# Ones for the warm-up, and V's first weights on ScalarE's queue: a transformer block of layer norm, sliding-window attention and a gated MLP

## The chip, the cores and the metric

The kernel runs on one core of a Trainium2 chip. The time is device microseconds of one execution, from the first to the last instruction; "before" is the median of three runs. The core has five engines with an instruction stream each: TensorE (PE, matmuls; its weight loads are listed as PEld), VectorE (DVE), ScalarE (ACT), GpSimd (POOL) and SyncE (SP), which here only issues DMA transfers. SBUF is the on-chip memory of 128 partitions, PSUM the memory into which TensorE accumulates, HBM the memory outside.

## The reference

For x of shape [1, 2048, 640] in bf16, with 32 heads of 20 channels and a window of 256 keys:

```python
def reference(A_x, A_wqkv, A_wo, B_x, B_w_gate, B_w_up, B_w_down):
    x = A_x
    xn = _layernorm(x, axis=-1)                  # mean, variance, eps 1e-5
    # _A_ref: q, k, v = xn @ wqkv;  scores = q k^T * Dh**-0.5
    #         mask: 0 <= i - j < 256;  softmax;  (p @ v) @ wo
    # _B_ref: h = sigmoid(xn @ w_gate) * (xn @ w_up);  h @ w_down
    return x + _A_ref(xn, A_wqkv, A_wo) + _B_ref(xn, B_w_gate, B_w_up, B_w_down)
```

Attention and MLP both read the same normalised rows, and the input is added to their sum.

## The kernel before

The sequence is worked through in four chunks of 512 rows, each of four blocks of 128 rows. Only the start of the kernel is touched by the change: the loads of chunk 0, the warm-up, the layer norm of chunk 0 and its V projection. First the warm-up tile and the loads, all on SyncE's queue, in program order:

```python
    warm = stp.tile([P, CW], BF16, name="st")          # 128 x 512
    nc.vector.memset(warm, 0.0)
    ...
    def load_rows(s, queue):                            # one block of x, 160 KB
        queue.dma_start(out=xc[0][:, s, :], in_=xr[:, s, :])

    def load_v(hf):                                     # 320 columns of wqkv, 400 KB
        a = 2 * D + hf * HALF
        nc.sync.dma_start(out=wqkv[:, :, a:a + HALF], in_=wqkv_r[:, :, a:a + HALF])

    load_rows(0, nc.sync)
    load_rows(1, nc.sync)
    load_v(0)
    load_rows(3, nc.sync)
    load_rows(2, nc.sync)
    load_v(1)
    load_wqkv(0)
    load_wqkv(1)
```

Then come constants, a first activation (so that ScalarE's table is loaded early) and ten matmuls of 128 x 512, whose result nobody reads. They keep TensorE busy until the first data are there:

```python
    make_identity(nc, ident)
    ...
    nc.scalar.activation(out=scr, in_=eps, func=SQRT)
    for n in (6, 4):
        ps = ps_d.tile([P, CW], FP32, name="pwarm", tag="d")
        for k in range(n):
            nc.tensor.matmul(ps, lhsT=warm[:, 0:P], rhs=warm, start=(k == 0), stop=(k == n - 1))
```

The layer norm of chunk 0 is shared by two engines. VectorE makes the statistics of blocks 0 and 2, ScalarE those of blocks 1 and 3; ScalarE takes every square root, VectorE every normalisation. TensorE transposes a normalised block by five matmuls with the identity, VectorE copies the result out of PSUM, and five matmuls of 320 columns project half of V for that block. The order below is the order of each engine's own stream:

```python
    mv0 = ln_block(0, 0)                 # VectorE: statistics of block 0
    xn1, neg1 = mean_act(1)              # ScalarE: mean of block 1
    r0 = root(mv0)                       # ScalarE: square root for block 0
    r1 = root_act(1, xn1, neg1)          # ScalarE: squares and root for block 1
    norm(0, mv0, r0)                     # VectorE: reciprocal, normalise block 0
    for lo, hi in ((0, 3), (3, DC)):
        transpose_rows(0, dve, lo, hi)   # TensorE transposes, VectorE copies
    v00 = project_v(0, 0, 0)             # TensorE: first half of V, block 0
    norm_act(1, xn1, neg1, r1)           # VectorE: normalise block 1
    xn3, neg3 = mean_act(3)
    r3 = root_act(3, xn3, neg3)
    half2 = ln_half(0, 2, 0)
    transpose_rows(1, dve)
    mv2 = ln_mv(ln_half(0, 2, 1, half2))
    v10 = project_v(0, 1, 0)             # first half of V, block 1
    copy_v(0, 0, 0, v00, act)
    r2 = root(mv2)
    v01 = project_v(0, 0, 1)             # second half of V, block 0
    norm_act(3, xn3, neg3, r3)
    norm(2, mv2, r2)
    ...                                  # blocks 3 and 2, then Q and K of chunk 0
```

After this, Q, K, the MLP, the scores and the products with V follow as one list of matmuls into which the attention steps are mixed.

Of the kernel before, what the change touches and what calls it, by code (L numbers as in the profile page):

```python
# [9 lines left out]
P = 128  # L10
# [7 lines left out]
CW = 512  # L18
# [6 lines left out]
HALF = 320  # L25
# [9 lines left out]
BF16 = mybir.dt.bfloat16  # L35
# [72 lines left out]
def kernel(  # L108
# [11 lines left out]
    nc = tc.nc  # L120
# [4 lines left out]
    def pool(name, bufs, **kw):  # L125
        return ctx.enter_context(tc.tile_pool(name=name, bufs=bufs, **kw))
# [5 lines left out]
    stp = pool("stp", 5)  # L132
# [23 lines left out]
    wqkv = const.tile([P, DC, 3 * D], BF16, name="wqkv")  # L156
    wqkv_r = A_wqkv.rearrange("(c p) n -> p c n", p=P)
# [2 lines left out]
    wd = const.tile([P, FC, D], BF16, name="wd")  # L160
    wo = const.tile([P, DC, D], BF16, name="wo")

    warm = stp.tile([P, CW], BF16, name="st")
    nc.vector.memset(warm, 0.0)
    def load_wqkv(part):
        nc.sync.dma_start(out=wqkv[:, :, part * D:(part + 1) * D],
                          in_=wqkv_r[:, :, part * D:(part + 1) * D])
# [3 lines left out]
    def load_rows(s, queue):  # L171
        queue.dma_start(out=xc[0][:, s, :], in_=xr[:, s, :])  # L172

    def load_v(hf):
        a = 2 * D + hf * HALF
        nc.sync.dma_start(out=wqkv[:, :, a:a + HALF], in_=wqkv_r[:, :, a:a + HALF])

    load_rows(0, nc.sync)
    load_rows(1, nc.sync)
    load_v(0)  # L180
    load_rows(3, nc.sync)
    load_rows(2, nc.sync)
    load_v(1)
    load_wqkv(0)
    load_wqkv(1)

# [49 lines left out]
    for n in (6, 4):  # L236
        ps = ps_d.tile([P, CW], FP32, name="pwarm", tag="d")
        for k in range(n):
            nc.tensor.matmul(ps, lhsT=warm[:, 0:P], rhs=warm, start=(k == 0), stop=(k == n - 1))


    xnT = {}
# [542 lines left out]
```

## Time and profile before

| | us |
|---|---|
| median of three runs | 313.3 |
| lowest, highest | 313.13, 313.94 |
| span in the profile | 311.7 |
| TensorE busy | 306.7 (98%) |
| ScalarE busy | 192.1 (62%) |
| VectorE busy | 159.9 (51%) |
| GpSimd busy | 155.5 (50%) |

In the views that follow, a line of the timeline has the start in us, the length in us, the engine, the line of the kernel and its operation, what it writes and reads with shapes, and in brackets how long the engine stood idle before and who ended that. Several instructions of one line that follow one another are merged, with their number after an x. A line of the chain has the start, the length and the work. SPq and ACTq are the issuing of transfers by SyncE and ScalarE. Matmuls are pipelined, so one matmul's length is more than the distance to the start of the next. Line 172 of the kernel loads a block of x, 176 half of V's weights, 239 is the warm-up, 248 and 254 are VectorE's statistics, 599 to 605 those of ScalarE, 589 the root, 268 and 610 the normalisations, 275 and 276 the transposes and their copies, 322 the V projection, 295 Q and K.

### The profile page before, as it was taken

What the parts mean: (1) busy time and instruction counts of PE and PEld (TensorE: products, weight loads), DVE (VectorE), ACT (ScalarE), POOL (GpSimd) and SP (SyncE); (2) the same over time, 40 slices, a digit from 0 to 9 for tenths busy, and PEclk for the clock granted to TensorE, in tenths of its full rate; (3) what the DMA queues carried; (4) which work ended last, traced back from release to release, by engine and by line L of the source; (5) the groups of instructions that cost most, each with busy time, mean ns of one, the idle gap of its engine ahead of it and who ended that gap; (6) DMA issues with size and microseconds to landing.
All of it is one profiled execution on the core that took longest, in us unless ns stands there. A gap on an engine that the chain in (4) does not pass through costs nothing.

```text
span 311.7 us, 10549 instructions
## 1 busy us (share of the span) xinstructions
PE 306.7 (98%) x4663; PEld 175.7 (56%) x4663; DVE 159.9 (51%) x315; ACT 192.1 (62%) x178; POOL 155.5 (50%) x239
## 2 busy tenths in 40 slices
PE   8999999999999999999999999999999999999996
PEld 3654444556557655644567665644556675444774
DVE  4533746648695264289826155262723526272423
ACT  5614787697764648787673647768585547778000
POOL 3000676576872827567382627546372845556000
PEclk9999999999999999999999999999999999999999
DMA  7995999574663153630025212730000223000002
GB/s 200 370 366 166 310 381 196 210 187 133 207 79 106 44 157 98 211 107 2 2 44 86 87 57 91 224 116 2 2 3 2 67 64 109 0 4 0 4 21 65
DMA packets 37614, 35.71 MB, mean 115 GB/s; under 512 B 10272, under 2 KB 37024, under 8 KB 37536
## 3 DMA queue, kind: packets, MB, share of 16 engines
q1 hardware_dynamic: 37280, 34.92, 38.5%
q8 instruction: 36, 0.59, 0.8%
q10 hardware_dynamic: 288, 0.11, 0.1%
q14 instruction: 10, 0.08, 0.1%
HBM read 23.63 MB, written 10.26 MB: 109 GB/s over the span
## 4 chain that ended last, share of the span: by engine, by line
PE 97%; DMA 2%; DVE 0%; SPq 0%; issue 0%; DVEq 0%
PE y L422 17%; PE pu L408 17%; PE pg L401 17%; PE pqk L295 14%; PE ps L472 9%; PE pv L322 7%; PE y L429 7%; PE acc L504 7%; DMA wqkv<-in_A_wqkv_dram 2%; PE pt L275 0%; SPq L172 0%; DVE h L412 0%; DVE xnT L276 0%; DVE xn L433 0%; DVEq L412 0%
## 5 line engine op out<-in xcount | busy, mean ns | idle before, releaser
L480 POOL TENSOR_SCALAR_AFFINE_SELECT pT<-pT 128x512 bf16<-128x512 bf16 (+2 forms) x192 | 147.0, 796 | 129.1 <-ACT pT L477 129.0
L477 ACT ACTIVATE pT<-ps 128x2048 bf16<-128x2048 f32 x76 | 142.7, 1878 | 64.0 <-PE ps L472 59.4
L412 DVE SCALAR_TENSOR_TENSOR h<-th,pu 128x512 bf16<-128x512 f32 x48 | 32.6, 682 | 60.5 <-PE pu L408 47.5
L408 PE MATMUL pu<-xnT,wu 128*128 128x512 bf16 x240 | 59.8, 380 | 0.0
L401 PE MATMUL pg<-xnT,wg 128*128 128x512 bf16 x240 | 59.8, 380 | 0.0
L422 PE MATMUL y<-wd,h 128*128 128x320 bf16 (+2 forms) x396 | 57.0, 296 | 0.0
L295 PE MATMUL pqk<-xnT,wqkv 128*128 128x512 bf16 x200 | 46.0, 381 | 0.0
L422 PEld LDWEIGHTS <-h 128*128 128x128 bf16 x396 | 36.5, 98 | 14.3
L404 ACT ACTIVATE th<-pg 128x512 f32<-128x512 f32 x48 | 28.6, 596 | 14.6 <-PE pg L401 14.3
L401 PEld LDWEIGHTS <-wg 128*128 128x128 bf16 x240 | 22.3, 98 | 25.3 <-issue 0.2
L408 PEld LDWEIGHTS <-wu 128*128 128x128 bf16 x240 | 21.9, 98 | 25.5 <-issue 0.6
L472 PEld LDWEIGHTS <-kT 20*64 20x64 bf16 x1856 | 20.6, 104 | 24.2 <-issue 22.3
L295 PEld LDWEIGHTS <-wqkv 128*128 128x128 bf16 x200 | 22.5, 119 | 18.0 <-issue 0.6
L472 PE MATMUL ps<-qT,kT 20*64 20x128 bf16 (+4 forms) x1856 | 32.5, 239 | 0.0
L433 DVE SCALAR_TENSOR_TENSOR rows<-y,rows 128x320 bf16<-128x320 f32 x30 | 14.5, 489 | 33.3 <-PE y L429 30.0
L514 DVE STREAM_TRANSPOSE t<-acc 128x512 f32<-128x512 f32 x32 | 22.0, 710 | 18.5 <-PE acc L504 18.2
L526 DVE TENSOR_TENSOR on<-t,rec 128x320 bf16<-128x320 f32 (+4 forms) x48 | 27.5, 573 | 1.1
L322 PE MATMUL pv<-wqkv,xnT 128*128 128x320 bf16 x160 | 23.9, 302 | 0.8 <-DVE xnT L276 0.6
L429 PE MATMUL y<-wo,oc 128*128 128x320 bf16 (+2 forms) x165 | 24.2, 295 | 0.0
L504 PE MATMUL acc<-pT,v 128*32 128x64 bf16 (+3 forms) x1376 | 23.2, 223 | 0.1
L504 PEld LDWEIGHTS <-v 128*32 128x32 bf16 x1376 | 18.6, 97 | 7.9 <-issue 1.9
L322 PEld LDWEIGHTS <-xnT 128*128 128x128 bf16 x160 | 15.0, 99 | 7.5 <-DVE xnT L276 1.3
(45 smaller groups left out, 134.0 us busy)
## 6 DMA issues: line engine op xcount, KB each, us to landing
qT<-sq SPq DMA_DIRECT2D x7, 512.0 KB, 5.9
sq<-st SPq DMA_DIRECT2D x20, 128.0 KB, 3.0
sk<-st SPq DMA_DIRECT2D x20, 128.0 KB, 3.1
rows<-in_A_x_dram SPq DMA_DIRECT2D x15, 160.0 KB, 2.3
out_dram<-rows SPq DMA_DIRECT2D x15, 160.0 KB, 1.8
kT<-sk SPq DMA_DIRECT2D x4, 512.0 KB, 6.4
wg<-in_B_w_gate_dram SPq DMA_DIRECT2D x2, 960.0 KB
wu<-in_B_w_up_dram SPq DMA_DIRECT2D x2, 960.0 KB, 9.9
```

Of the source, the lines that this page charges most:

```text
L295: nc.tensor.matmul(ps, lhsT=wt[:, m, :], rhs=xnT[c][:, d, :], start=(d == 0), stop=(d == DC - 1))
L322: nc.tensor.matmul(ps[:, 0:HALF], lhsT=xnT[c][:, d, s * P:(s + 1) * P], rhs=wqkv[:, d, 2 * D + hf * HALF:2 * D + (hf + 1) * HALF], start=( ...
L401: nc.tensor.matmul(pg, lhsT=part(wg, d, f), rhs=xnT[c][:, d, :], start=(d == 0), stop=(d == DC - 1))
L404: nc.scalar.activation(out=th, in_=pg, func=TANH, scale=0.5)
L408: nc.tensor.matmul(pu, lhsT=part(wu, d, f), rhs=xnT[c][:, d, :], start=(d == 0), stop=(d == DC - 1))
L412: nc.vector.scalar_tensor_tensor(out=h, in0=th, scalar=1.0, in1=pu, op0=ADD, op1=MULT)
L422: nc.tensor.matmul(y[:, 0:cut[1] - cut[0]], lhsT=ht[c, f][:, s * P:(s + 1) * P], rhs=wd[:, f, cut[0]:cut[1]], start=(f == 0), stop=False)
L429: nc.tensor.matmul(y[:, 0:cut[1] - cut[0]], lhsT=oc[c, m][:, s * P:(s + 1) * P], rhs=wo[:, m, cut[0]:cut[1]], start=False, stop=(m == DC - 1))
L472: nc.tensor.matmul(ps[hf * U:(hf + 1) * U, i, col * U:(col + n) * U], lhsT=qk["k", kc, g // GH][32 * i:32 * i + DH, g % GH, key:key + U], ...
L477: nc.scalar.activation(out=pt[:, :, 0:CW], in_=ps, func=EXP, scale=SCALE)
L480: nc.gpsimd.affine_select(out=out, in_=in_, pattern=[[0, HG], [0, n], [sign, width]], compare_op=GE, fill=0.0, base=base, channel_multipli ...
L504: nc.tensor.matmul(acc[32 * i:32 * i + 32, q * U:(q + n) * U], lhsT=v[:, h * VW:h * VW + 32], rhs=pt[:, i, col * U:(col + n) * U], start=( ...
```

## The change

Two things are done at the start of the kernel. The warm-up matmuls read a constant of ones that the program has anyway, one element per partition read again for every column, in place of a tile that VectorE must first clear; so they have nothing of their own to wait for. And the first half of V's weights is issued by ScalarE, as its first instruction, beside SyncE's issue of the first block of x, and not as the third transfer on SyncE's queue; the first V projection is to have its weights sooner. The other transfers stay on SyncE in the same order.

```diff
-    warm = stp.tile([P, CW], BF16, name="st")
-    nc.vector.memset(warm, 0.0)
+    ones = nc.const_aps.tensor(1.0, [P, CW], BF16)
...
-    def load_v(hf):
+    def load_v(hf, queue):
         a = 2 * D + hf * HALF
-        nc.sync.dma_start(out=wqkv[:, :, a:a + HALF], in_=wqkv_r[:, :, a:a + HALF])
+        queue.dma_start(out=wqkv[:, :, a:a + HALF], in_=wqkv_r[:, :, a:a + HALF])

     load_rows(0, nc.sync)
     load_rows(1, nc.sync)
-    load_v(0)
+    load_v(0, nc.scalar)
     load_rows(3, nc.sync)
     load_rows(2, nc.sync)
-    load_v(1)
+    load_v(1, nc.sync)
     load_wqkv(0)
     load_wqkv(1)
...
-            nc.tensor.matmul(ps, lhsT=warm[:, 0:P], rhs=warm, start=(k == 0), stop=(k == n - 1))
+            nc.tensor.matmul(ps, lhsT=ones[:, 0:P], rhs=ones, start=(k == 0), stop=(k == n - 1))
```

## The prediction

> **What bounds the kernel now.** I read the page first: the shares of busy time, the forty slices and the chain of work that ended last.
>
> ```profile
> PE 306.7 (98%) x4663; PEld 175.7 (56%) x4663; DVE 159.9 (51%) x315; ACT 192.1 (62%) x178; POOL 155.5 (50%) x239
> PE   8999999999999999999999999999999999999996
> DMA  7995999574663153630025212730000223000002
> PE 97%; DMA 2%; DVE 0%; SPq 0%; issue 0%; DVEq 0%
> ```
>
> TensorE is busy for 306.7 of 311.7 us and carries 97% of the chain. Nothing in the change touches those matmuls. What is not TensorE on the chain lies in the first slices, so the second view is the chain of the first 40 us, in order of time (start, length, what).
>
> ```profile
> 0.80 0.40 SPq L172
> 1.25 0.42 SPq L172
> 1.72 4.72 DMA wqkv<-in_A_wqkv_dram
> 6.47 1.19 PE pv L322 x5
> 7.66 0.29 PE pt L275 x5
> 7.98 0.50 DVE xnT L276
> 8.53 1.53 PE pv L322 x10
> 14.01 10.79 PE pqk L295 x50
> ```
>
> The first useful TensorE work that isn't a transpose is V's first half for block 0, at 6.47 us. The chain gives its wait to V's first 400 KB, issued third on SyncE's queue at 1.72 and landing 4.72 us later, at 6.44. From 8.53 us on TensorE hardly stops: from 8.50 to 13.85 it is busy 5.33 of 5.35 us. So the end moves almost one for one with the start of this dense stretch at 8.53. Third view: the timeline of the first microseconds, for what else ends just before 6.47.
>
> ```profile
> 0.92 0.27 DVE L164 MEMSET st<- 128x256 uint32 x1 [0.92 <-PEq L769]
> 1.25 4.45 PE L239 MATMUL pwarm<-st 128*128 128x512 bf16 x10 [1.25 <-DVE st L164]
> 3.13 0.88 DVE L248 BATCH_NORM_STATS2 stats<-xc 128x6 f32<-128x320 bf16 x2 [1.94 <-DMA xc<-in_A_x_dram]
> 3.63 0.74 ACT L599 ACTIVATE xn<-xc 128x640 bf16<-128x640 bf16 x1 [0.63 <-DMA xc<-in_A_x_dram]
> 4.37 0.28 ACT L589 ACTIVATE rstd<-mv,eps 128x1 f32<-128x1 f32 x1
> 4.88 0.45 DVE L268 TENSOR_SCALAR xn<-xc,mv,rstd 128x640 bf16<-128x640 bf16 x1
> 5.50 0.74 PE L275 MATMUL pt<-ident,xn 128*128 128x128 bf16 x5
> 6.06 0.55 DVE L276 COPY xnT<-pt 128x384 bf16<-128x384 bf16 x2 [0.73 <-PE pt L275]
> 6.47 0.85 PEld L322 LDWEIGHTS <-xnT 128*128 128x128 bf16 x5 [0.51 <-DVE xnT L276]
> 6.47 1.19 PE L322 MATMUL pv<-wqkv,xnT 128*128 128x320 bf16 x5 [0.24 <-DMA wqkv<-in_A_wqkv_dram]
> ```
>
> The last two lines are the point. The weight load of the same matmul also starts at 6.47, and it waited 0.51 us for the transposed block from VectorE. The matmul has two releasers which come within a few hundredths of each other: V's landing (6.44) and the layer norm of x's first block. Removing one leaves the other.
>
> That second chain starts with x, not with V. Block 0 lands by 3.13, block 1 by 3.63. ScalarE works in order: it takes the mean of block 1 (3.63, with its accumulator read out from 4.27) ahead of the root of block 0 (4.37). The statistics of block 0 were there at about 4.26 (the aggregate is 0.21 long from 4.05). So the root is released by whichever is later of block 0 plus some 1.2 us and block 1 plus 0.74 us, and just now these are nearly equal as well. Then root, reciprocal, normalisation, transposes and copy take 4.37 to 6.42.
>
> [...] Here an issue of V's half costs SyncE 0.43 us and one of x some 0.42 (four issues, median 424 ns)[...]. [...] the warm-up matmuls are 0.43 us apart (weight loads at 2.08, 2.51, 2.94), while 50 matmuls of the same 512 columns take 10.79 us later, 0.216 each. The switch is seen at V's first five: they start at 6.47, 6.71, 6.98, 7.22 and 7.36, so from 0.24-0.27 to 0.14 apart at about 7.2 us.
>
> **The change part by part.** (a) The memset of 0.27 us on VectorE goes. Nothing else on VectorE waits behind it until 3.13: worth nothing by itself.
>
> (b) The warm-up reads a constant that GpSimd writes at 0.37, ahead of the barrier at which the engines start (0.80 on SyncE and ScalarE). The ten matmuls can start at about 0.85 instead of 1.25, and end their issue at 0.85 + 10 x 0.427 = 5.1 instead of 5.5. Before, the first transpose (its weights loaded at 5.38) stood behind the last warm-up until 5.50; that is up to 0.1 us to gain. An earlier start may also bring the warm clock forward by up to 0.4 us[...]. At most it saves the cold half of what lies between 5.5 and 7.2: three transposes ahead of the first copy (3 x 0.05 us: five cold ones take 0.74 us with a last one of 0.31, so they start 0.107 apart; five at 7.50 take 0.44 with a last one of 0.22, so 0.055) and three V matmuls (3 x 0.12): up to 0.5 us, but only the first 0.15 lies on the way to 8.53, since block 1's normalisation on VectorE waits for block 0's copies, not for V. Taken with the 0.1: -0.1 to -0.25. Against it: if layer norm comes later, TensorE is idle from 5.1 to about 6[...].
>
> (c) V's first half is issued at 0.80 on ScalarE instead of 1.72 on SyncE, 0.92 us earlier, and the issues behind it on SyncE move up by about 0.47 (0.43 and a gap). It should land near 5.0 to 5.7 (estimate: 4.72 us from issue, or less without two blocks ahead of it). As layer norm releases the matmul at the same 6.47, this gains less than 0.05. ScalarE pays 0.43 us of issue ahead of its table load (0.80 to 2.08, then to about 2.5); its next work waits for GpSimd until 2.79 anyway, so nothing.
>
> (d) What it costs: [...] In the stretch 3.10 to 5.40 the DMA engines are already at 0.88 and 238 GB/s, in 1.25 to 3.10 at 0.63 although nothing moved at first. So x's blocks slip. If half of the turns go to V, block 0's 160 KB, which take about 0.54 us at the 302 GB/s of the stretch 6.50 to 8.50, take about 0.8 (V's packets are half as long as x's): +0.3; block 1 has that twice, +0.6. I take +0.3 for block 0 and +0.5 for block 1. The root of block 0 then waits for block 1's mean: 4.37 + 0.5 = 4.87.
>
> (e) Blocks 3 and 2 and V's second half land earlier (ScalarE waits 1.14 us for block 3 at 6.92, VectorE 0.18 us for block 2). But after 8.53 TensorE waits for none of them: nothing.
>
> Sum: +0.5 (d), -0.15 (b, chosen near the middle), 0 for (a), (c), (e): about +0.35 us at 8.53, carried to the end. 313.3 + 0.35 = 313.65; I say 313.6.
>
> **The rivals.** First, V really was the releaser and x doesn't slip (the early ramp at 0.63 leaves room for the 400 KB): then V's half gives up its few hundredths and the clock comes earlier, for -0.2 to -0.5 us, 312.8 to 313.1. For it: the chain names the DMA, and the engines weren't full before 3.1. Against: the weight load's own wait for VectorE. Second, the hole in TensorE's work keeps the array cold for another window: 3.4 us of work of which about 80% is matmul at half rate loses 1.4 us; with the slip, 315. For it: two of the three inputs (an earlier end of warm-up, a later x) point this way; against: five transposes and the V matmuls fill part of the hole, and in before a pause of 0.24 us did no harm. Third, the transfer is hidden and all cancels: 313.3.
>
> **Range and chances.** The three times before lie between 313.13 and 313.94, so 0.4 us is noise. The cases: slip with some clock gain, 50%, 313.3 to 314.0; gain, 30%, 312.8 to 313.2; cold window, 15%, to 315. The range 312.7 to 314.6 holds 8 in 10. Two per cent are 6.3 us, more than the whole time before V's first matmul could give up: faster 0.01, same 0.98, slower 0.01.
>
> **What would show each step.** In the profile after: the warm-up starts at 0.8 to 0.9 (b). V's first half lands before 5.8 and the first V matmul waits for VectorE, not for the DMA (c). The first statistics start at 3.3 to 3.5 and block 1's mean on ScalarE near 4.1 (d); if they still start at 3.13 and 3.63, the slip is wrong. The dense stretch starts at 8.8 to 9.0 instead of 8.53. V's first matmuls 0.24 apart throughout would show the cold window. I'd be wrong altogether if the end moved by more than the dense start did, by a rearrangement later that I don't foresee.

## The result, and the profile after

The changed kernel takes 316.7 us (median of six runs, 316.04 to 318.45), the kernel before 313.47 beside it (313.13 to 313.94). The ratio is 1.0108, with a 95% interval of 1.0079 to 1.0137: slower by about 1.1%, less than the 2% of the three chances, but outside the range that was predicted. (This ratio and those below come from the runs' own comparison; they are not exactly the quotient of the medians.)

The page of the changed kernel, the same rows as for before and the clock row (its program has one line fewer, so line numbers are one lower):

```profile
PE 305.5 (97%) x4627; PEld 175.9 (56%) x4663; DVE 159.6 (51%) x314; ACT 192.4 (61%) x178; POOL 155.5 (49%) x239
PE   6999999999999999999999999999999999999995
PEclk9799999999999999999999999999999999999999
DMA  8976999746655152640025212640000223000001
PE 95%; DMA 1%; issue 1%; DVE 1%; ACT 0%; SPq 0%; DVEq 0%
```

TensorE's first slice fell from 8 to 6 tenths, and the clock row has a 7 in the second slice, where before it had nothing but nines. (36 matmul records are missing from this trace, 4627 against 4663, so TensorE's busy time looks shorter, and the chain shows small pieces of "issue" where they are missing.) The rest of the page is as before, so the start is where to look. The chain of the first microseconds (start, length, what):

```profile
1.25 3.76 DMA xc<-in_A_x_dram
...
5.04 0.83 ACT xn L598 x2
5.87 0.19 ACT rstd L588
...
6.29 0.46 DVE xn L267
...
7.58 0.85 PE pv L321 x5
...
9.37 2.85 PE pv L321 x10
12.22 0.43 PE pt L274 x5
```

V's weights have left the chain, and block 1 of x has taken their place: it is issued at 1.25 as before, but is there only at 5.01. Then the same steps follow as before, all later, until the second group of V matmuls starts at 9.37 (before: 8.53). That group then takes 2.85 us where it took 1.53. Ahead of the first transposes TensorE stood idle for 1.53 us, since the warm-up was over and block 0 was not yet normalised; this is the hole that the following sections speak of:

```profile
6.79 0.45 PE L274 MATMUL pt<-ident,xn 128*128 128x128 bf16 x5 [1.53 <-DVE xn L267]
```

Why the second group is slow is in the stretches of the changed kernel, cut where the clock changed, with the 3.41 us ahead of the first change (columns: length, busy time and number of instructions on TensorE, weight load, VectorE, ScalarE and GpSimd, granted clock as a share of the full one, share of the DMA engines, GB/s):

```profile
2.18:5.59 3.41, 3.08 (x8) 0.77 (x6) 1.09 (x3) 1.14 (x3) 1.14 (x12) 1.00 1.04 330
5.59:9.00 3.41, 1.66 (x15) 0.97 (x15) 2.26 (x8) 3.31 (x11) 0.00 (x0) 1.00 1.06 366
9.00:12.42 3.42, 3.05 (x14) 1.90 (x15) 1.91 (x7) 1.39 (x5) 0.00 (x0) 0.50 1.07 370
12.42:16.16 3.74, 3.74 (x34) 2.82 (x32) 1.48 (x3) 1.57 (x5) 0.00 (x0) 1.00 1.06 374
```

From 5.59 to 9.00 TensorE was busy for 1.66 us of 3.41; the next 3.41 us ran at half clock, just when the dense stretch began. (The 1.00 of the first row is no measurement: the clock's records begin at 5.59, and the warm-up matmuls before it are 0.43 us apart.)

The difference of the two profiles, 314.4 - 311.7 = 2.7 us, adds up from three places. The dense stretch starts 0.84 later (9.37 against 8.53). Q starts at 16.16 against 13.85, 2.31 later, so 1.47 came on top in the window of half clock. From there to the last matmul nothing is added (the chain's last five matmuls start at 310.77 against 308.52, 2.25 later). The last 0.4 us lie behind the last matmul and are told of at the end.

### The profile page after: what moved, and what is told of

It reads as the page before. It is cut to its first block, busy times and chain, and to the rows that moved or that the text cites. A ratio compares the mean times of both kernels' runs of the same rounds, so it can differ in the third digit from the quotient of the medians.

```text
span 314.4 us, 10512 instructions
## 1 busy us (share of the span) xinstructions
PE 305.5 (97%) x4627; PEld 175.9 (56%) x4663; DVE 159.6 (51%) x314; ACT 192.4 (61%) x178; POOL 155.5 (49%) x239
## 4 chain that ended last, share of the span: by engine, by line
PE 95%; DMA 1%; issue 1%; DVE 1%; ACT 0%; SPq 0%; DVEq 0%
PE y L421 17%; PE pu L407 17%; PE pg L400 17%; PE pqk L294 14%; PE ps L471 9%; PE pv L321 8%; PE y L428 7%; PE acc L503 7%; DMA xc<-in_A_x_dram 1%; PE pt L274 0%; DVE xnT L275 0%; ACT xn L598 0%; DVE h L411 0%; DVE xn L267 0%; SPq L171 0%
## 5 line engine op out<-in xcount | busy, mean ns | idle before, releaser
L400 PE MATMUL pg<-xnT,wg 128*128 128x512 bf16 x225 | 57.8, 380 | 1.0 <-issue 0.5
L321 PE MATMUL pv<-wqkv,xnT 128*128 128x320 bf16 x160 | 24.9, 310 | 0.9 <-DVE xnT L275 0.9
```

The costliest lines, as they stand in the source:

```text
L321: nc.tensor.matmul(ps[:, 0:HALF], lhsT=xnT[c][:, d, s * P:(s + 1) * P], rhs=wqkv[:, d, 2 * D + hf * HALF:2 * D + (hf + 1) * HALF], start=( ...
L400: nc.tensor.matmul(pg, lhsT=part(wg, d, f), rhs=xnT[c][:, d, :], start=(d == 0), stop=(d == DC - 1))
```

## The experiments

Theory A: V's packets go ahead of block 1 of x, ScalarE's root waits for block 1, and the hole that this leaves in TensorE's work brings half clock. Theory B, the rival: ones, or the earlier start of the warm-up, cost time through the clock. Within A it was open whether V delays block 1 by taking turns on the DMA engines or by being served first.

| run | median us | before beside it | ratio, 95% interval |
|---|---|---|---|
| e1 ones only | 314.23 | 314.22 | 1.0003 (0.9985 to 1.0020) |
| e2 V on ScalarE's queue only | 317.38 | 314.22 | 1.0101 (1.0068 to 1.0135) |
| e3 one queue, V ahead of block 1 | 318.00 | 314.22 | 1.0112 (1.0083 to 1.0142) |
| e4 changed kernel, 14 warm-ups | 315.04 | 314.22 | 1.0033 (1.0023 to 1.0043) |
| e5 block 1 ahead of V on ScalarE's queue | 313.72 | 314.04 | 0.9998 (0.9979 to 1.0016) |
| e6 half of the gate weights early | 317.30 | 314.04 | 1.0079 (1.0054 to 1.0105) |
| e7 e5 and e6 | 314.64 | 314.04 | 1.0040 (1.0021 to 1.0058) |
| e8 loads as before, 6 warm-ups | 316.14 | 314.04 | 1.0051 (1.0034 to 1.0069) |
| e9 before, MLP weights ahead of small loads | 313.41 | 314.01 | 0.9978 (0.9963 to 0.9993) |
| e10 e5, 12 warm-ups, move of e9 | 313.13 | 314.01 | 0.9962 (0.9947 to 0.9976) |
| e11 e4 and move of e9 | 314.79 | 314.01 | 1.0026 (1.0012 to 1.0040) |

**e1 and e2: each half of the change alone.**

```diff
 # e1, against the changed kernel
-    load_v(0, nc.scalar)
+    load_v(0, nc.sync)
 # e2, against the changed kernel
-    ones = nc.const_aps.tensor(1.0, [P, CW], BF16)
+    ones = stp.tile([P, CW], BF16, name="st")
+    nc.vector.memset(ones, 0.0)
```

> Ones for the warm-up, V's first half back as third transfer on SyncE's queue. Theory A (the loss comes from V's packets standing ahead of x's block 1, and from the hole this leaves in TensorE's work): block 1's mean starts near 3.63 us again, the dense stretch near 8.5, and the time is that of before, 313.2 to 313.8. Theory B (ones in place of zeros, or the earlier warm-up, costs the time through the clock): the time stays near 316 with block 1 on time.

> V's first half on ScalarE's queue, the warm-up on zeros from VectorE as before. Theory A: block 1 lands near 5.0 us as in the changed kernel, the dense stretch starts near 9.4, and most or all of the loss is there: 315.5 to 317. Theory B: near 313.5 to 314.4, the slip alone.

e1 is as fast as before, e2 as slow as the changed kernel. Theory B is out: within the 0.2% of the interval, some 0.6 us, the ones cost nothing and gain nothing. In the timelines, block 1's mean on ScalarE, first of e1, then of e2:

```profile
3.61 0.74 ACT L598 ACTIVATE xn<-xc 128x640 bf16<-128x640 bf16 x1 [0.62 <-DMA xc<-in_A_x_dram]
```

```profile
5.22 0.74 ACT L599 ACTIVATE xn<-xc 128x640 bf16<-128x640 bf16 x1 [2.22 <-DMA xc<-in_A_x_dram]
```

e1's median lies above the top of its expected range, but so did before's on that chip; the comparison is the ratio.

e1's timeline also shows V's weights binding for once. The array ran at full clock before the first transposes (the clock's records begin at 4.20; the five transposes took 0.46 where before's took 0.74), so block 0's transposed rows came earlier, at 6.16, and the first V matmul then waited until 6.65 for V, still third on SyncE's queue:

```profile
6.16 0.10 PEld L321 LDWEIGHTS <-xnT 128*128 128x128 bf16 x1 [0.51 <-DVE xnT L275]
6.65 0.84 PE L321 MATMUL pv<-wqkv,xnT 128*128 128x320 bf16 x5 [0.82 <-DMA wqkv<-in_A_wqkv_dram]
```

Block 1's transposes stand behind these matmuls, so the dense stretch starts at 8.46, only 0.07 ahead of before. An earlier V can be worth something once the full clock comes earlier; no run has both and x on time.

**e3: turns, or order?** SyncE issues everything, in the order block 0, V, block 1.

```diff
     load_rows(0, nc.sync)
+    load_v(0, nc.sync)
     load_rows(1, nc.sync)
-    load_v(0, nc.scalar)
```

> All on SyncE's queue, but in the order x block 0, V's first half, x block 1; ones for the warm-up. If the second queue matters only by the order that it brings about (theory A1), block 1 lands at 5.0 to 5.5 us and the time is 316 to 317.5. If two rings[...] are the cause (theory A2, contention), block 0 lands near 3.1 as before, block 1 is some 1 us late at most since V's 400 KB follow one another, and the time is under 315.5.

The loss is there without a second queue, so the order of issue alone is enough for it. Block 1's mean comes later still, after the 5.0 to 5.5 that I expected, and 318.0 lies above 316 to 317.5; the clock's records show half clock for 6.83 us, from 8.00 to 14.82, twice as long as in the changed kernel:

```profile
5.85 0.74 ACT L598 ACTIVATE xn<-xc 128x640 bf16<-128x640 bf16 x1 [2.85 <-DMA xc<-in_A_x_dram]
```

The packets of the changed kernel say the same: from 3.00 to 3.75 us 415 packets of V (640 bytes each, ScalarE's queue) start and a single one of x; x's packets come back at 3.85, when V's are almost through (its landing is complete at 4.57, block 1's at 5.02). V did not take turns with block 1, it went before it. With block 0 it overlapped: from 2.50 to 3.00 us 70 packets of x and 85 of V start.

**e4: fill the hole.** The changed kernel with four more warm-up matmuls.

```diff
-    for n in (6, 4):
+    for n in (8, 6):
```

> The changed kernel with 14 warm-up matmuls in place of 10: the slip of block 1 stays, the hole in TensorE's work before the first transposes (5.1 to 6.8 us) shrinks by 0.9 to 1.7 us. Theory A: no window of half clock after the warm-up, the loss falls from 3.2 us to the slip's 0.9 to 1.3: 314.2 to 315.0. If the hole isn't the cause of the cold window: 316 to 317 as in the changed kernel.

Measured 1.0033, two thirds of the loss gone with four matmuls that compute nothing. Block 1 is still late, but the second group of V matmuls is quick again; the timeline of e4:

```profile
0.84 5.54 PE L238 MATMUL pwarm<-const-bfloat16-1.0 128*128 128x512 bf16 x14 [0.84 <-PEq L768]
6.59 0.45 PE L274 MATMUL pt<-ident,xn 128*128 128x128 bf16 x5 [0.21 <-DVE xn L267]
7.38 0.85 PE L321 MATMUL pv<-wqkv,xnT 128*128 128x320 bf16 x5 [0.34 <-DVE xnT L275]
9.17 1.53 PE L321 MATMUL pv<-wqkv,xnT 128*128 128x320 bf16 x10 [0.59 <-DVE xnT L275]
```

The wait for the normalised block shrank from 1.53 us, in the changed kernel, to 0.21. In the window of 3.41 us that begins at 5.63, where e4's clock records begin, TensorE was busy for 2.40 us, against 1.66 in the changed kernel's from 5.59, and no half clock followed. The dense stretch starts 0.64 later than before, yet e4's profile is 313.8, 2.1 above before's: 0.4 of it lies behind the last matmul, and something else waited. Its list of waits names it (who waited, for whom: us, times, longest):

```profile
PEld L407 <- DMA wu<-in_B_w_up_dram: 1.1, 1, 1.1
PE pu L407 <- DMA wu<-in_B_w_up_dram: 1.0, 1, 1.0
```

The second half of the MLP's up weights lands at about the time of its first use near 41 us. e1's profile has 0.5 us of the same wait, the profiles of before and of the changed kernel none.

**e5: the same queues, the other order.** ScalarE issues block 1 and then V.

```diff
     load_rows(0, nc.sync)
-    load_rows(1, nc.sync)
+    load_rows(1, nc.scalar)
     load_v(0, nc.scalar)
```

> The changed kernel with x's block 1 issued by ScalarE ahead of V's first half (ScalarE: block 1, V; SyncE: blocks 0, 3, 2 and the rest). If the order in which transfers are issued decides who is served first, block 1 lands by 3.7 us although V stays on ScalarE's queue, V lands by 5.7, the dense stretch starts at 8.2 to 8.6 and the time is that of before, within 0.5 us. If V on a second queue hurts in itself, the dense stretch starts after 9 and the time is 1 us or more above before.

The time is that of before, within 0.2%: behind block 1, V on ScalarE's queue does no harm that the runs show. The chain of e5 is bound by block 0 now, which lands 0.6 us later than before, beside block 1:

```profile
0.80 2.93 DMA xc<-in_A_x_dram
...
3.75 0.90 DVE stats L247 x2
...
8.53 1.53 PE pv L321 x10
```

So what is gained on block 1 is lost on block 0, and the dense stretch starts at 8.53 as before. Here two queues were served side by side: from 2.50 to 3.25 us 99 packets of SyncE's queue and 111 of ScalarE's start, and blocks 0 and 1 both land late, at 3.73 and 3.91. Block 1's mean began at 3.93, not by 3.7 as I expected. Two of its 18 runs took over 316.4; I come back to them with e10.

**e8: the hole alone.** Ones, loads as before, but six warm-up matmuls instead of ten.

```diff
-    for n in (6, 4):
+    for n in (3, 3):
```

> All loads as before, ones for the warm-up, but 6 warm-up matmuls in place of 10: the hole in TensorE's work ahead of the first transpose grows from near nothing to about 2 us without any transfer moved. If such a hole is by itself enough for a window of half clock: block 1 on time near 3.63 us, yet V's second group of ten matmuls takes over 2 us where it took 1.5, and the time is 0.5 to 1.8 us above before. If the hole matters only beside the moved transfer: as before.

No transfer has moved, and 0.5% is lost. The timeline of e8:

```profile
0.83 2.72 PE L238 MATMUL pwarm<-const-bfloat16-1.0 128*128 128x512 bf16 x6 [0.83 <-PEq L768]
5.42 0.71 PE L274 MATMUL pt<-ident,xn 128*128 128x128 bf16 x5 [1.86 <-DVE xn L267]
6.37 1.51 PE L321 MATMUL pv<-wqkv,xnT 128*128 128x320 bf16 x5 [0.24 <-DVE xnT L275]
9.00 2.60 PE L321 MATMUL pv<-wqkv,xnT 128*128 128x320 bf16 x10 [0.58 <-DVE xnT L275]
```

From layer norm up to 6.37 the starts are within 0.1 us of before's. Here the array didn't fall back to half clock, it stayed there until 11.21, where before's switched at 7.19. So a shorter warm-up, with the hole of 1.86 us that it leaves, is enough to prolong the half clock without any transfer moved; the falling back itself is what the changed kernel and e4 show.

**e6 and e7: the up weights earlier, first try.** Half of the gate weights (960 KB) is moved from after the small loads to before the first of them, in e6 on top of e1, in e7 of e5.

```diff
-            load_gu(k)
+            load_gu(k, ((wu, B_w_up),))      # in load_rest: only the up weights are left
...
             if w == "k" and m == 1:
+                if c == 0:
+                    load_gu(1, ((wg, B_w_gate),))
                 spread("q", c, 0, GH if c else 2)
```

> Ones for the warm-up, all loads on SyncE in the order of before; the second half of the gate weights (960 KB) issued ahead of the first load of q's transposed rows, at about 24 us in place of 30. Theory: a second transfer, the second half of the up weights, lands within a few tenths of a us of its use near 40.6 us and adds a wait of 0 to 1.1 us that differs from run to run. Then the wait of pu for wu near 40 us is gone, and the time falls by 0.3 to 1.0 us below before. If the scores then wait for k's rows instead (issued behind the 960 KB): no gain or a loss of up to 1 us.

> The two edits of e5 and e6 together: block 1 ahead of V on ScalarE's queue, and the second half of the gate weights early. If both waits are independent the gains add: 0.3 to 1.3 us below before.

Both are slower, e6 by more than the 1 us that I had allowed for: in their profiles nothing waits for the up weights, but TensorE waits for k's rows, 2.4 us in e6 and 0.9 in e7. The waits of e6:

```profile
PEld L473 <- DMA kT<-sk: 2.9, 1, 2.9
PE ps L473 <- DMA kT<-sk: 2.4, 1, 2.4
```

e6's clock records show half clock from 33.71 to 37.12, right behind this wait (in the 3.41 us before, TensorE was busy for 1.02): the same two-step loss, in another place.

**e9, e10 and e11: second try.** The MLP's weights are issued one step earlier only, ahead of 384 KB that the scores need last.

```diff
             spread("k", c, 0, 1)
             spread("k", c, 1, 3)
-            spread("q", c, 2, 4)
-            spread("k", c, 3, 4)
 ...                             # in load_rest, behind load_gu(1)
+        spread("q", 0, 2, 4)
+        spread("k", 0, 3, 4)
```

> The kernel before (zeros, all loads on SyncE in the old order), with one move: the second halves of the gate and up weights are issued ahead of two small loads of transposed rows (q groups 2 and 3, k group 3: 384 KB), which the scores first need at 42.9 us. If the up weights' landing near 40 us adds a wait that differs from run to run (0 in the profile of before, 0.5 in that of e1, 1.1 in that of e4), it goes: the times bunch at the low end of before's, and the median falls by 0.3 to 0.8 us. If before doesn't wait there in most runs: no difference.

> e5 (ones; ScalarE issues block 1 and then V's first half) with 12 warm-up matmuls in place of 10, so that TensorE is busy up to the first transpose near 5.95 us, and with the move of e9. Both losses gone: the dense stretch at 8.3 to 8.6 us, no run in a cold window, no wait for the up weights: 0.3 to 1.0 us below before. If the moves change nothing: as before.

> e4 (the changed kernel with 14 warm-up matmuls) with the move of e9. What e4 lost against before beyond the slip of 0.6 us at the dense stretch was a wait for the up weights: it goes, and 0 to 0.5 us above before remain. If e4's rest has another cause: 1 us above before, as e4.

e9 gains 0.2% on before with this move alone. That fits a wait for the up weights in many runs of before, though before's profile has none. e10 beats both kernels: 0.9962 (0.9947 to 0.9976), and its 22 runs lie between 312.98 and 313.49, where the 59 runs of before beside it spread from 313.06 to 316.62. The intervals of e9 and e10 overlap, so what e10's other edits add to the move is not shown by the medians. None of its runs has e5's 316, but why is open: in its profile the clock rose at 3.76, the twelve warm-ups were over at 5.03 and left a hole of 0.89 us, more than e5's 0.68. Only at half clock throughout would they last to about 5.96 (estimate, 0.84 + 12 x 0.427). The two long runs of e5 have a mean clock of 1.000. A first switch that came late, as e8's at 11.21, would fit, since e8's records begin with it; no profile of them was taken.

e11 falls to 314.79, 1.7 above e10, and doesn't reach the 0 to 0.5 above before that I expected. Its profile has no wait for the up weights and is 1.4 us longer than e10's: the dense start is 0.73 later (9.23 against 8.50), of which 0.5 is left at the last matmul, and the last store lands 0.9 later (below). So the slip has a price of its own, and the late store is the part that I had not counted.

## Why the prediction was wrong

The changed kernel was predicted at 313.6 in 312.7 to 314.6; it takes 316.7.

**What failed is step (d), and with it the weight of a rival.** It supposed that half of the turns go to V, an estimate that no trace of before showed, and came to "+0.3 for block 0 and +0.5 for block 1". The path was right: the root of block 0 waited for block 1's mean. Mis-sized was block 1's slip, 1.41 (3.63 to 5.04) in place of 0.5, since block 1 stood behind nearly all of V (the packets; e3 and e5 for the order). Block 0 slipped by 0.33 (3.13 to 3.46), as sized, but that was luck: in e2 and e4, with the same loads, its statistics start at 3.17 and 3.15. The traces don't decide whether two queues take turns: e5 has them side by side (99 and 111 packets start from 2.50 to 3.25), the changed kernel has V all but alone from 3.00 to 3.75 (415 packets against one). Why block 1 got no turn there stays open.

**The second rival came true.** "The hole in TensorE's work keeps the array cold for another window" had 15%, and its size (1.4 us) was right: 1.47 in the profile, where the half clock lasted for one window. But it was set beside the slip as an alternative, when it follows from it. With a slip of 1.41 the hole was 1.53 us, and a window that was busy for 1.66 of 3.41 us was followed by half clock. In the other profiles, windows of that length at full clock with 1.76 us (e2), 0.81 (e3) and 1.02 (e6) were also followed by half clock, those with 2.02 (e1), 2.19 (e5) and 2.40 (e4) were not. The rival's 3.4 us for a window was in no trace of before; the changed kernel's clock records show the length (full clock from 5.59, half from 9.00, full again from 12.42, 3.41 us apart). The changed kernel's six runs lose different amounts; they have mean clocks of 0.995 (316.04 to 316.26), 1.000 (317.14) and 0.987 to 0.989 (317.39 and 318.45). One window of 3.41 us at half rate in 314 us takes 0.005 off the mean, two take 0.011 (e3's profile, with 6.83 us, has 0.987), so the last two had about two (estimate). The run at 1.000 isn't explained; a late first switch would look like this (e8's records begin with its switch at 11.21, and its profile has 1.000).

**(b)** The warm-up started at 0.84 as predicted; its -0.15 is too small for the runs to tell (e1: 1.0003, give or take 0.002). In the changed kernel it could not come, since the first transposes waited for x; in e1's profile 0.07 of it reached the dense start, because V then bound. **(c)** was right in the changed kernel: V landed at 4.57, even earlier than 5.0 to 5.7, and the first V matmul waited for VectorE. But it was sized without (b): with the early clock of e1, V was 0.49 us later than the rows that it meets (6.65 against 6.16). **(e)** was right. The first rival fell here, as x did slip. "Carried to the end" held only from 16 us on, where what was lost is still there at the last matmul, within 0.06 us. The sign that I had named for being wrong altogether came true: the end moved by 2.7 us, the dense start by 0.84.

## What to carry to other kernels

When two transfers are wanted at the start, ask which one the longest chain hangs on: a transfer that has slack (V) must not be issued ahead of one that has none (x's block 1), and here a second queue didn't take it out of the line (block 1 slipped by 1.41 us). A late start of the first matmuls was paid twice here, once as itself (0.84 us) and once in the clock (1.47 us). So let warm-up matmuls run until the first real ones can start, with a margin, and count a hole behind them as a risk: the changed kernel's, of 1.53 us, was followed by 3.41 us of half clock, and e3's profile has 6.83 us of it. Where a landing and its use fall within half a microsecond of each other, as for the up weights, look at the spread of the runs and not at one profile.

## What the runs showed of the hardware that I had not expected

V's 400 KB took less time in the changed kernel, 3.77 us from issue to complete landing (0.80 to 4.57) against 4.72 in before (1.72 to 6.43), though it was issued beside a block of x. One of its packets took some 32 ns from 3.00 us on, where before it took 40 to 57 between 3.25 and 4.75. Part of it is order: in before V's first packet starts at 2.92, behind two blocks of x, in the changed kernel at 2.37. Why each packet took less time is open.

The last store's landing, counted from the start of the last matmul, is complete after 2.29 us in before, 2.73 in the changed kernel, 2.93 in e11 and 2.04 in e5 and e10, for the same store. In the changed kernel a packet of 8,192 bytes on an instruction queue starts 1.57 us after the last matmul, beside the store's packets, which end at 2.08; in e10 it starts at 2.09, when they are through (1.70). Of the thirteen profiles, the three in which such a packet comes only behind the store's (e5, e7, e10) have 2.04 to 2.05 us, the other ten 2.29 to 3.00. So a packet on an instruction queue may delay a store by some tenths of a microsecond, and these three, with one more transfer issued by ScalarE, happen to shift it; this was seen in the records and not tried.
